# Load order, the queue of one load, and the source of the scaled identities at the start of a fused attention and feed-forward kernel

## Chip, cores, metric

One core of one Trainium2 chip. The metric is the device time of one execution in microseconds (us), as the median of several executions; lower is better. All executions told here count as fast in the record: none is over 1.5% above the fastest of its kernel.

## The reference, cut

```python
# q, k, v: (4, 8, 768, 64) fp32;  w_in: (512, 2048);  w_out: (2048, 512)
scores = scale * q @ k.T + (-slopes[h] * dist)     # ALiBi; window of 96 keys back, plus the 8 first keys
a = softmax(where(keep, scores, -1e9))
x = (a @ v).transpose(0, 2, 1, 3).reshape(3072, 512)
h = x @ w_in
out = (relu(h) ** 2) @ w_out                       # (3072, 512) fp32
```

## The kernel before

The sequence is cut into 24 tiles of 128 rows (T0 to T23), the feed-forward part into 12 blocks of two tiles with 8 steps each. A planner in the kernel's Python code decides at build time in which order each engine gets its operations, from estimated landing times. GpSimd issues nearly all loads, and they convert fp32 to bf16 on the way; SyncE loads the q and k of tile 0 in plain fp32. The weights come in 8 pieces each: i0 to i7 (w_in, named `win`) and o0 to o7 (w_out, named `wout`), 256 KB apiece in bf16.

```python
    issue = [1.0, 5.0]                     # the planner's estimate of issue and landing of the loads
    ...
    for j in range(NPLAIN):                # tile 0 only
        for n, src in ((0, q), (1, k)):
            t_ = const([P, d_model], FP32, f"plain_{n}{j}")
            nc.sync.dma_start(...)         # plain q, then plain k
            land["qk"[n], j] = 4.15 + 1.1 * n
    ...
    nc.gpsimd.iota(pbi, pattern=[[-P, 2], [-1, P]], base=0, channel_multiplier=1)
    load_part(0, 1)                        # q of tile 1, by GpSimd
    load_part(1, 1)                        # k of tile 1
    load_v(0)
    load_v(1)
    nc.scalar.activation(junk, zero[:, :1], Act.Exp)      # first exponential, result unused
    ...
    nc.vector.tensor_scalar(ident, pbi[:, 0, :], 0.0, None, op0=Alu.is_equal)   # bf16 identity
    ...
    for h in range(H):                     # 8 heads: identity times slope, the ALiBi term for TensorE
        nc.vector.tensor_scalar_mul(sid[h], ident, float(slopes[h] / scale))
    ...
    for w in "i0 T2 i1 T3 i2 o0 i3 o1 i4 o2 T4 i5 o3 i6 o4 T5 i7 o5 o6 o7".split():
        kind, n = w[0], int(w[1:])
        {"T": load_tile, "i": load_w_in, "o": load_w_out}[kind](n)     # T: q, k and v of a tile
    ...
    # last block: ScalarE copies each finished output part from PSUM, SyncE stores it
    nc.scalar.copy(o_sb[:, cols], acc);  nc.sync.dma_start(out=out[rows, cols], in_=o_sb[:, cols])
```

(The last line is condensed.)

The softmax here doesn't subtract the row's maximum and nothing guards it: scores larger than these inputs give would overflow.

Of the kernel before, what the change touches and what calls it, by code (L numbers as in the profile page):

```python
# [15 lines left out]
Alu = mybir.AluOpType  # L16
# [83 lines left out]
def kernel(  # L100
# [11 lines left out]
    nc = tc.nc  # L112
# [14 lines left out]
    scale = 1.0 / math.sqrt(D)  # L127
    slopes = [2.0 ** (-8.0 * (h + 1) / H) for h in range(H)]
# [20 lines left out]
    def const(shape, dt, name):  # L149
        return consts.tile(shape, dt, name=name, tag=name)  # L150
# [7 lines left out]
    ident = const([P, P], BF16, "ident")  # L158
# [3 lines left out]
    pbi = const([P, 2, P], I32, "pbi")  # L162
    pb = const([P, 2, P], BF16, "pb")
    pb0 = const([P, P], BF16, "pb0")
    sid = [const([P, P], BF16, f"sid_{h}") for h in range(H)]
# [10 lines left out]


    land = {}
    issue = [1.0, 5.0]

    def landed(name, at):
        land[name] = plan.op(("land",) + name, {"DMA": 0.0}, None, ready=at)
# [1 line left out]
    def slot(j):  # L184

        return j if j < NFIRST + 2 else NFIRST + 2 + j % NQ

    def src_rows(x, j):
        b, t = divmod(j, TPB)
        return x[b, :, t * P : (t + 1) * P, :]  # L190

    def swdge(name, dst, src, t):
        nc.gpsimd.dma_start(out=dst, in_=src)  # L193
        issue[1] = max(issue[1], issue[0] + 3.3) + t
        issue[0] += 0.75 if name[0][0] == "w" else 0.88

        land[name] = issue[1] + 0.3 + min(max(0.1 * (issue[1] - 8), 0.0), 1.6)

    plain = {}
    for j in range(NPLAIN):  # L200
        for n, src in ((0, q), (1, k)):
            t_ = const([P, d_model], FP32, f"plain_{n}{j}")
            nc.sync.dma_start(
                out=t_.rearrange("p (h d) -> p h d", h=H),
                in_=src_rows(src, j).rearrange("h p d -> p h d"),
            )
            plain[n, j] = t_
            land["qk"[n], j] = 4.15 + 1.1 * n


    def load_v(j):
        swdge(("v", j), v_sb[j][:, :, :D], src_rows(v, j).rearrange("h p d -> p h d"), 0.97)

    def load_part(n, j):
        swdge(
            ("qk"[n], j), qk_ring[slot(j)][:, n, :].rearrange("p (h d) -> p h d", h=H),
            src_rows((q, k)[n], j).rearrange("h p d -> p h d"), 0.85,
        )
# [6 lines left out]
    def load_w_in(s):  # L225
        f = slice(s * 2 * P, (s + 1) * 2 * P)
        swdge(
            ("win", s), w_in_sb[s],
            moe_w_in[:, f].rearrange("(km p) f -> p km f", p=P), 1.3,
        )  # L230
# [10 lines left out]
    def emit_ones(e, js):  # L241
        for j in js:
            nc.vector.memset(v_sb[j][:, :, D : D + 1], 1.0)

    emit_ones(None, range(NFIRST + 2))
    nc.gpsimd.iota(pbi, pattern=[[-P, 2], [-1, P]], base=0, channel_multiplier=1)  # L246
    load_part(0, 1)
    load_part(1, 1)
    load_v(0)
    load_v(1)  # L250

    nc.scalar.activation(junk, zero[:, :1], Act.Exp)

# [16 lines left out]
    nc.vector.memset(pb[:n_global, 1, :], float(-n_local))  # L270
    nc.vector.tensor_scalar_max(pb0[:n_global, :], pb0[:n_global, :], float(-n_local))
    for h in range(H):
        nc.vector.tensor_scalar_mul(sid[h], ident, float(slopes[h] / scale))
    for g in range(2):
        for odd in range(2):
            for i in range(2):
# [5 lines left out]
    for g in range(NFIRST + 2, NT, 6):  # L282
        js = range(g, min(g + 6, NT))
        o = plan.op(
            ("ones", g), {"DVE": 0.2}, lambda e, js=js: emit_ones(e, js),
            key=-1.0, ready=15.0,
        )
        ones.update({j: o for j in js})

    for w in "i0 T2 i1 T3 i2 o0 i3 o1 i4 o2 T4 i5 o3 i6 o4 T5 i7 o5 o6 o7".split():  # L290
        kind, n = w[0], int(w[1:])
        {"T": load_tile, "i": load_w_in, "o": load_w_out}[kind](n)
    for name, at in list(land.items()):
        landed(name, at)

# [36 lines left out]
    for j in range(NT):  # L332
# [61 lines left out]
        if j >= JQK:  # L394
            def emit_dT(e, j=j, T_=T_):
# [5 lines left out]
            T = plan.op(  # L401
                ("T", j), {"SP": 1.3}, emit_dT,
                deps=[land["q", j], land["k", j], xT_op[j - 3]] + ku, key=base - 6,
            )
            T = plan.op(("moved", j), {"DMAQ": 1.2}, None, deps=[T])
# [56 lines left out]
        for gs in [(0,), (1,)] if j < NSPLIT and not first else [tuple(range(groups))]:  # L462
            n = 8 * len(gs)
# [3 lines left out]
            if j < NBIAS:  # L467
# [6 lines left out]
            o = plan.op(  # L474
                ("sc", j, gs[0]), {"PE": 0.2 + 0.029 * n},
                lambda e, gs=gs, f=emit_sc: f(e, gs), deps=[*deps, bias],
                key=base + 1 + 2 * gs[0], takes=takes,
            )
# [237 lines left out]
    for o in plan.ops:  # L716
        if o["name"][0] == "sc":
            j = o["name"][1]
            n = 4 * j - LEAD
# [3 lines left out]
    for blk in range(NBLK):  # L723
# [9 lines left out]
        for s, sub, half in order2:  # L733
            users = acc_users.setdefault((sub, half), [])
            w = d_model if half is None else d_model // 2
# [3 lines left out]
            def emit_s2(e, blk=blk, s=s, sub=sub, half=half, w=w, cols=cols, own=own):  # L739
# [15 lines left out]
            o = plan.op(  # L755
                ("s2", blk, s, sub), {"PE": 0.43 * w / d_model}, emit_s2,
                deps=[d, land["wout", s]] + users[-1:],
                key=8 * blk + s + 2.0 + (0 if not last else 8 * sub + 8 * (half or 0)),
                takes=((*G, [users]) if own else ("acc", NACC, [users])) if s == 0 else None,
            )  # L760
# [71 lines left out]
```

## Time and profile before

| | before |
|---|---|
| time, median of 6 executions beside the changed kernel | 215.16 us (214.77 to 215.30) |
| span of the profiled execution | 213.1 us |
| TensorE busy | 205.5 us (96%) |
| last weight piece, o7, has landed | 41.97 us |
| last matmul ends | 209.96 us |
| from there to the end of the span | 3.1 us |

Times within a trace start at the span's start. A load's landing is when the last of its 16 DMA engines has finished. First the timeline of GpSimd in the kernel before (start, length, engine, line, operation, tiles): the jobs in which GpSimd writes the descriptors (the transfer orders for the DMA engines) for the v of tiles 0 and 1, joined into one row.

```profile
3.22 2.37 POOL L193 DMA_DIRECT2D v<-in_v_dram  x2
```

One by one in the trace, the first of the two took 1.50 us and the second 0.88. Then, in the DMA view, the 2.8 us that begin 0.34 us after the last matmul of before (210.3 to 213.1 us, the end of the span): the last store, 128 KB, by queue (packets, MB, share of the 16 engines), and its time from issue to landing.

```profile
q1 hardware_dynamic: 144, 0.13, 14.0%
...
out_dram<-o SPq DMA_DIRECT2D x1, 128.0 KB, 1.7
```

Nothing else uses the DMA engines there, and the store lands after 1.7 us.

### The profile page before, as it was taken

What the parts mean: (1) busy time and instruction counts of PE and PEld (TensorE: products, weight loads), DVE (VectorE), ACT (ScalarE), POOL (GpSimd) and SP (SyncE); (2) the same over time, 40 slices, a digit from 0 to 9 for tenths busy, and PEclk for the clock granted to TensorE, in tenths of its full rate; (3) what the DMA queues carried; (4) which work ended last, traced back from release to release, by engine and by line L of the source; (5) the groups of instructions that cost most, each with busy time, mean ns of one, the idle gap of its engine ahead of it and who ended that gap; (6) DMA issues with size and microseconds to landing.
All of it is one profiled execution on the core that took longest, in us unless ns stands there. A gap on an engine that the chain in (4) does not pass through costs nothing.

```text
span 213.1 us, 5046 instructions
## 1 busy us (share of the span) xinstructions
PE 205.5 (96%) x1992; PEld 141.2 (66%) x1992; DVE 142.4 (67%) x383; ACT 117.5 (55%) x217; POOL 74.4 (35%) x91
## 2 busy tenths in 40 slices
PE   7968999999999999999999999999999999999994
PEld 3656677655676767666767667666767667676773
DVE  7756668752886768755867957855857857844640
ACT  6848476633763645753654754753754754733541
POOL 8986677531044134314314422422422400000000
PEclk9999999999999999999999999999999999999999
DMA  9999999999899999999999899799999992310202
GB/s 127 140 165 197 182 196 182 178 123 210 185 95 87 218 100 93 189 129 84 203 141 81 180 103 119 154 128 119 192 130 78 152 131 39 123 28 0 98 0 98
DMA packets 113702, 27.58 MB, mean 129 GB/s; under 512 B 104336, under 2 KB 110736, under 8 KB 113680
## 3 DMA queue, kind: packets, MB, share of 16 engines
q0 software_dynamic: 79200, 13.37, 81.4%
q1 hardware_dynamic: 34480, 13.90, 32.7%
q8 instruction: 15, 0.25, 0.5%
q14 instruction: 7, 0.06, 0.1%
HBM read 27.26 MB, written 6.29 MB: 157 GB/s over the span
## 4 chain that ended last, share of the span: by engine, by line
PE 87%; DMA 7%; POOL 4%; issue 0%; ACT 0%; POOLq 0%
PE hT L675 39%; PE acc L745 38%; DMA win<-in_moe_w_in_dram 7%; PE sc L449 5%; PE po L562 4%; POOL qk L193 2%; POOL v L193 1%; PE tr L372 0%; POOL win L193 0%; PE trx L625 0%; ACT o L304 0%; POOL pbi L246 0%; POOLq L246 0%; POOLq L813 0%
## 5 line engine op out<-in xcount | busy, mean ns | idle before, releaser
L675 PE MATMUL hT<-xT,win 128*128 128x256 bf16 x768 | 98.7, 273 | 0.4 <-DMA win<-in_moe_w_in_dram 0.2
L745 PE MATMUL acc<-wout,hs 128*128 128x512 bf16 (+1 forms) x400 | 98.1, 371 | 0.2 <-DMA wout<-in_moe_w_out_dram 0.2
L696 ACT ACTIVATE hr<-hT 128x512 f32<-128x512 f32 x96 | 57.4, 599 | 68.1 <-PE hT L675 67.0
L675 PEld LDWEIGHTS <-win 128*128 128x128 bf16 x768 | 72.8, 98 | 23.9 <-DMA win<-in_moe_w_in_dram 1.6
L708 DVE TENSOR_TENSOR hs<-hr 128x512 bf16<-128x512 f32 x96 | 65.9, 687 | 23.0 <-ACT hr L696 21.7
L745 PEld LDWEIGHTS <-hs 128*128 128x128 bf16 x400 | 36.5, 98 | 24.4 <-issue 0.4
L193 POOL DMA_DIRECT2D qk<-in_q_dram x23 | 20.6, 894 | 87.0 <-DVE qk L346 75.0
L495 ACT ACTIVATE esc<-sc 128x512 bf16<-128x512 f32 x78 | 42.1, 601 | 10.3 <-PE sc L449 10.3
L520 DVE TENSOR_TENSOR at<-esc,E 128x512 bf16<-128x512 bf16 x78 | 32.0, 422 | 8.0 <-ACT esc L495 6.9
L193 POOL DMA_DIRECT2D v<-in_v_dram x24 | 22.2, 924 | 2.4 <-DVE at L520 1.2
L590 DVE TENSOR_TENSOR x<-po,rs 128x256 bf16<-128x256 f32 x48 | 20.4, 425 | 1.7
L193 POOL DMA_DIRECT2D qk<-in_k_dram x23 | 20.5, 892 | 0.3 <-issue 0.2
L562 PEld LDWEIGHTS <-at 128*128 128x128 bf16 x352 | 16.8, 97 | 4.5 <-ACT at L495 0.6
L562 PE MATMUL po<-v,at 128*128 128x65 bf16 x352 | 18.6, 193 | 0.3 <-ACT at L495 0.3
L589 DVE RECIPROCAL rs<-po 128x4 f32<-128x4 f32 x48 | 8.7, 181 | 13.2 <-PE po L562 13.0
L449 PEld LDWEIGHTS <-qkT 64*128 64x128 bf16 x352 | 9.9, 94 | 8.4 <-issue 6.6
L306 DVE COPY o<-acc 128x512 f32<-128x512 f32 x11 | 7.6, 692 | 10.6 <-PE acc L745 10.6
L449 PE MATMUL sc<-qkT 64*128 64x128 bf16 x192 | 13.1, 219 | 0.4 <-DVE qkT L306 0.3
L304 ACT COPY o<-acc 128x512 f32<-128x512 f32 (+1 forms) x14 | 7.8, 555 | 6.7 <-PE acc L745 6.7
L449 PE MATMUL sc<-qkT,qkT 64*128 64x128 bf16 x160 | 11.3, 216 | 0.0
L193 POOL DMA_DIRECT2D win<-in_moe_w_in_dram x8 | 6.4, 794 | 1.7 <-DMA win<-in_moe_w_in_dram 1.1
L495 ACT ACTIVATE at<-sc 128x512 bf16<-128x512 f32 x10 | 5.3, 598 | 2.5 <-PE sc L449 2.5
(41 smaller groups left out, 58.2 us busy)
## 6 DMA issues: line engine op xcount, KB each, us to landing
out_dram<-o SPq DMA_DIRECT2D x23, 256.0 KB, 3.1
v<-in_v_dram POOLq DMA_DIRECT2D x24, 128.0 KB, 5.6
qk<-in_q_dram POOLq DMA_DIRECT2D x23, 128.0 KB, 4.7
qk<-in_k_dram POOLq DMA_DIRECT2D x23, 128.0 KB, 5.4
win<-in_moe_w_in_dram POOLq DMA_DIRECT2D x8, 256.0 KB, 8.6
wout<-in_moe_w_out_dram POOLq DMA_DIRECT2D x8, 256.0 KB, 8.8
qkT<-qk SPq DMA_TRANSPOSE x18, 3.5
xT<-x SPq DMA_TRANSPOSE x18, 3.8
```

The source lines that it names most:

```text
L193: nc.gpsimd.dma_start(out=dst, in_=src)
L304: nc.scalar.copy(dst, src)
L449: nc.tensor.matmul(out=tiles["sc", j, odd, g][:, at, :], lhsT=qkT[(j - kt) % NKT][half, 1, pair, :], rhs=qkT[j % NKT][half, 0, pair, :], s ...
L495: nc.scalar.activation(out=esc, in_=tiles.pop(("sc", j, odd, g)).rearrange("p a c -> p (a c)"), func=Act.Exp, scale=scale,)
L520: nc.vector.tensor_mul(at, tiles.pop(("esc", j, odd, g)), bias)
L562: nc.tensor.matmul(out=po[:, hi, :], lhsT=tiles["at", j, odd, g][:, at * P : (at + 1) * P], rhs=v_sb[kj][:, h, :], start=(i == 0), stop=(i ...
L589: nc.vector.reciprocal(rs, po[:, :, D : D + 1])
L590: nc.vector.tensor_tensor(out=x[:, 4 * hf : 4 * hf + 4, :], in0=po[:, :, :D], in1=rs.to_broadcast([P, 4, D]), op=Alu.mult,)
L675: nc.tensor.matmul(out=hT[:, c, :], lhsT=w_in_sb[s][:, kt, c * P : (c + 1) * P], rhs=tiles["xT", blk][:, kt, :], start=(kt == 0), stop=(kt ...
L696: nc.scalar.activation(hr, tiles.pop(("hT", blk, s)), Act.Relu)
L708: nc.vector.tensor_mul(hs, hr, hr)
L745: nc.tensor.matmul(out=tiles["acc", blk, sub, half], lhsT=hs[:, c, sub * P : (sub + 1) * P], rhs=w_out_sb[s][:, c, cols], start=(s == 0 an ...
```

## The change

Its intent: to have the first four tiles on the chip before all weights but one, so that TensorE has attention work early; to get the k of tile 0 a little sooner by issuing it from a second queue; and to make the scaled identities straight from the int32 distances. The diff without its comments and blank lines:

```diff
-    issue = [1.0, 5.0]
+    issue = [1.35, 4.6]
-        land[name] = issue[1] + 0.3 + min(max(0.1 * (issue[1] - 8), 0.0), 1.6)
+        land[name] = issue[1] + (0.5 if issue[1] < 8 else 0.8 if issue[1] < 13.6 else 1.7)
-        for n, src in ((0, q), (1, k)):
+        for n, src, eng in ((0, q, nc.sync), (1, k, nc.scalar)):
-            nc.sync.dma_start(
+            eng.dma_start(
-            land["qk"[n], j] = 4.15 + 1.1 * n
+            land["qk"[n], j] = 4.15 + 0.6 * n
-    load_part(0, 1)
-    load_part(1, 1)
-    load_v(0)
-    load_v(1)
-        nc.vector.tensor_scalar_mul(sid[h], ident, float(slopes[h] / scale))
+        nc.vector.tensor_scalar(
+            sid[h], pbi[:, 0, :], 0.0, float(slopes[h] / scale), op0=Alu.is_equal, op1=Alu.mult
+        )
-    for w in "i0 T2 i1 T3 i2 o0 i3 o1 i4 o2 T4 i5 o3 i6 o4 T5 i7 o5 o6 o7".split():
-        kind, n = w[0], int(w[1:])
-        {"T": load_tile, "i": load_w_in, "o": load_w_out}[kind](n)
+    pieces = {
+        "T": load_tile, "i": load_w_in, "o": load_w_out, "v": load_v,
+        "q": lambda j: load_part(0, j), "k": lambda j: load_part(1, j),
+    }
+    for w in "q1 k1 v0 v1 q2 k2 v2 q3 k3 i0 v3 i1 i2 o0 i3 i4 T4 i5 o1 i6 o2 i7 o3 T5 o4 o5 o6 o7".split():
+        pieces[w[0]](int(w[1:]))
```

The first four loads are the same in both; `issue` and `land` are estimates by which the planner orders the work. "The new order" below always means the new order of loads together with the new estimates for GpSimd's loads.

## The prediction

> **What bounds the kernel now.** I read the page from the top: busy shares, slices, chain; then the chain in order of time, the waits and single issues of the first 45 us.
>
> ```profile
> span 213.1 us, 5046 instructions
> PE 205.5 (96%) x1992; PEld 141.2 (66%) x1992; DVE 142.4 (67%) x383; ACT 117.5 (55%) x217; POOL 74.4 (35%) x91
> ...
> PE   7968999999999999999999999999999999999994
> ...
> DMA  9999999999899999999999899799999992310202
> ...
> PE 87%; DMA 7%; POOL 4%; issue 0%; ACT 0%; POOLq 0%
> ```
>
> PE is busy for 205.5 of 213.1 us. The missing 7.6 us lie at the start (second digit row: slices 1 to 4, some 21 us) and in the last 3 us, when the last output is stored. The chain of waits, in order of time, says what the start waits for:
>
> ```profile
> 1.35 1.90 POOL qk L193 x2
> 3.25 2.34 POOL v L193 x2
> 5.59 0.76 POOL win L193
> 6.34 1.76 POOL qk L193 x2
> 8.10 0.82 POOL v L193
> 8.92 7.17 DMA win<-in_moe_w_in_dram
> 16.37 8.80 DMA win<-in_moe_w_in_dram
> 25.22 1.92 PE hT L675 x16
> ```
>
> Columns are start, length, what. Up to 25.22 us the chain is loads; from there it is matmuls to the end. So the time is "25.2 us, plus the PE work still to do then". The busy time by stretch (PE first after the length) shows where PE is short of work:
>
> ```profile
> 9.00:11.00 2.00, 1.63 (x29) 1.03 (x28) 1.47 (x7) 1.92 (x4) 2.00 (x3) 1.00 1.94 167
> 11.00:14.00 3.00, 1.52 (x24) 1.35 (x25) 1.19 (x5) 0.59 (x1) 3.00 (x5) 1.00 2.01 175
> 14.00:17.00 3.00, 2.79 (x39) 2.15 (x37) 1.83 (x22) 2.25 (x5) 1.90 (x3) 1.00 2.17 163
> 17.00:19.00 2.00, 1.55 (x34) 1.20 (x32) 1.31 (x5) 1.29 (x3) 1.75 (x3) 1.00 1.38 202
> 19.00:25.20 6.20, 5.74 (x62) 3.48 (x56) 5.48 (x16) 3.67 (x8) 3.97 (x5) 1.00 1.51 195
> 25.20:42.50 17.30, 17.28 (x185) 13.23 (x186) 12.60 (x29) 11.89 (x22) 11.49 (x14) 1.00 1.74 183
> ```
>
> Idle: 0.37 + 1.48 + 0.21 + 0.45 + 0.46 = 2.97 us between 9 and 25.2, then 0.02. The largest hole, in the timeline of PE, is tile 2, whose q and k stand behind a weight:
>
> ```profile
> 11.99 0.40 PE L372 MATMUL tr<-ident,qk 128*128 128x128 bf16 x4 [1.08 <-DMA qk<-in_q_dram]
> 12.87 0.40 PE L372 MATMUL tr<-ident,qk 128*128 128x128 bf16 x4 [0.48 <-DMA qk<-in_k_dram]
> ```
>
> Busy PE hides more, because a lone group shows its pipeline latency (four transposes 0.40 us, but 0.22 us apart when back to back). Counting the work from 4.15 to 25.2 us at the pace of back-to-back groups gives 14.2 us in 21, so about 7 us of PE is unused there. That is all a better start could ever win (3%).
>
> The DMA queue is the second bound. Landing times (issue plus time to landing, one issue at a time): q1 6.1, k1 6.8, v1 about 9.0; i0 11.1, q2 11.9, k2 12.8, v2 13.8; i1 16.1, q3 17.0, k3 17.7, v3 18.8; i2 20.0, o0 21.2, i3 22.6, o1 23.9, i4 25.2, o2 26.5; T4 27.4 to 29.2; i5 30.4, o3 31.6, i6 32.9, o4 34.3; T5 35.2 to 37.0; i7 38.2, o5 39.5, o6 40.7, o7 42.0 (i and o are the 256 KB pieces of the two weights, T a tile's q, k and v). Steady pace: 0.9 us for a q, k or v, 1.3 for a weight piece. It never pauses up to 42 us, and PE consumes o5 at 39.48 and o6 at 40.73 us, within 0.1 us of their landing. So even the smooth stretch after 25 us runs at the heels of the loads. Reordering can shift PE work in front of a late piece; it cannot make the last piece come much earlier.
>
> **What the Trainium skill says.** "DMA: Bandwidth & Descriptors", section "Issuing engines are not separate DMA queues": DMAs started from different engines run on the same 16 engines and interleave, so a second issuer only saves issue time. The trace agrees as far as it goes: tile 0's plain q and k are issued 0.52 us apart and land at 3.9 and 5.2 us, 1.3 us apart, so transfer and not issue separates them. "SBUF — State Buffer", section "Who interferes with whom": a VectorE tensor_scalar in a two-port mode locks GpSimd out, which then cannot write descriptors, and whoever starts first blocks the other. The trace has a case that fits: the first of the eight identity scalings took 585 ns and the median is 176, beside a running descriptor job. "VectorE: DVE Perf Modes", section "The perf-mode tier table": tensor_scalar runs at 4x from bf16 and 2x from fp32, so the int32 input of the new form should not be faster; at 128 columns that is a small part of 176 ns.
>
> **The change part by part.**
>
> *k of tile 0 on ScalarE's queue.* It is issued 0.52 us sooner, but both transfers share the engines. Their 2048 packets start at 2.9 us and moved at about 1,075 per us in the trace, so both should land near 2.9 + 1.9 = 4.8 us: k 0.4 earlier, q 0.9 later. The first transposes move from 4.15 to about 4.85 us, the second from 5.16 to 5.35. ScalarE's issue (about 0.5 us) is hidden, since its exponentials wait for the mask until 3.3 us anyway. Worth -0.2 us locally; tile 1's loads (6.1 and 6.8 us) are behind it and absorb that. Zero at the end.
>
> *Scaled identities from the distances.* Same eight instructions, 8 x 176 ns plus one stall = 1.3 us, ending near 4.7 us in both; first needed at 5.5 us. Zero.
>
> *Order of loads.* It removes i0 from ahead of T2 and i1 from ahead of T3; i1 to i4 follow v3, T4 comes two pieces earlier, and o1, o2, o3 later. Two gains. First, tile 2's and 3's q and k are no longer behind weights. A part lands 4.6 us after its issue where GpSimd is the limit, and issues are 0.88 us apart from 5.57 us: q2 10.2, k2 11.1, v2 12.0, q3 12.9, k3 13.8 instead of 11.9, 12.8, 13.8, 17.0, 17.7. Second, the queue runs with fewer holes: i0 + T2 took 4.8 us (9.0 to 13.8) and i1 + T3 took 5.0, where the steady pace gives 1.3 + 2.7 = 4.0. Of the excess 1.8 us, one 16 KB instruction fetch that held one DMA engine for 945 ns at 14.7 us explains about 1, and it will come again; a hole of about 0.5 us before i0's first packets will not. I credit 0.5 us. So i0 lands near 16.0 (after: 5 us later than before), i1 18.2, i2 19.5, o0 20.8, i3 22.1, i4 23.4, q4 24.3, i5 27.4, o1 28.7, i6 30.0, o2 31.3, i7 32.6, o3 33.9, k5 35.6, o4 37.7, o5 39.0, o6 40.2, o7 41.5.
>
> Now PE's new order (the order of the instructions is decided when the kernel is built, and can be read) against these, with 0.87 us a step of the first product (s1), 0.86 a step of the second (s2), 0.22 a transpose group, 0.24 a pv group, 0.55 a score group. All of tile 2's and 3's scores are done by about 16.3 us, then s1 0 with i0 at 16.0 to 16.3, s1 1 at 18.3 (i1), s1 2 at 19.6 (i2), s2 0 at 20.9 (o0), s1 3 at 22.2 (i3), s1 of block 1, s1 4 at 23.9. In the old order s1 4 starts at 25.22, with the same total in front of it (one s1 more, one s2 less). Ahead by 1.3 us there. Then the loads catch up: s2 1 waits for o1, 28.8; s1 6 for i6, 30.1; s2 2 for o2, 31.4; s2 6 for o6, 40.3; s2 7 about 41.7 to 41.9. In the old trace s2 7 starts at 42.46 with 0.24 us less work ahead of it, so it corresponds to 42.70: ahead by 0.8 to 1.0 us. The old stretch from 25.2 to 42.5 contained 0.4 us of small bubbles that my walk leaves out, so I take 0.4 to 1.0, centre 0.7. After 42 us nothing is changed but a few neighbours' places. 215.3 - 0.7 = 214.6 us.
>
> **Rivals.** (1) *The last weights bound everything:* o6 and o7 land as before (40.7, 42.0), the start's idle time only moves, and the gain is 42.70 - 42.1 = 0.6 at most, likelier 0.2: 215.1. For it: PE takes o5 and o6 at their landing. (2) *The loads recover both excesses*, i1 to o7 land 1.1 us earlier, and PE follows: 213.8. For it: no weight among parts, no hole; against it: the instruction fetch. (3) *First product late:* i0 lands 5 us later and four s1 steps bunch behind 16 us; with too little attention work to fill, PE idles from 16.5 to 22 and the new order starts behind: 215.6. For it: s1 1, s1 2, s2 0 and s1 3 each wait for a landing in my walk. (4) *Attention at once fills the gap*, all 3 us of idle time gone: 212.5; against it the landings from 18 us on.
>
> **Range and chances.** The rivals span 213.8 to 215.6, centre 214.6; 8 in 10 for 213.9 to 215.3. Two per cent would be 4.3 us, more than all visible idle time before 25 us; nor does anything here cost that.
>
> **What would show it.** Right: waits for q2 and q3 shrink from 1.08 us to a few tenths; PE waits for win and wout between 16 and 32 us instead; i4 near 23.4; o7 near 41.5; the chain still loads first, then matmuls from some point between 20 and 42 us. Wrong: o7 a whole us earlier or later than 41.5, plain q still landing at 3.9, sid instructions longer than 0.3 us each, or a PE wait on ACT or VectorE that replaces the loads before 25 us.

## The result

The changed kernel took 215.56 us (215.49 to 216.72, 6 executions), the kernel before 215.16. The ratio is 1.0035, with a 95% interval of 1.0013 to 1.0056: not faster, but about 0.35% (0.75 us) slower. The predicted 214.6 and its range up to 215.3 miss it. (Ratios here are the mean time of one kernel's fast runs over that of the other's of the same rounds, so not quite the ratio of the medians quoted.) The profiled execution happened to be the slowest of the six, 216.72 us. A second run of the same kernel (e1_again) gave a profile at 215.28, which is typical.

The page of the changed kernel, top lines and chain:

```profile
span 214.9 us, 5049 instructions
PE 206.4 (96%) x1992; PEld 142.0 (66%) x1992; DVE 142.6 (66%) x384; ACT 117.3 (55%) x216; POOL 74.8 (35%) x91
...
PE   7988999899999999999999999999999999999992
...
DMA  8999999999796999997999999899999990310202
...
PE 82%; DMA 9%; POOL 6%; DVE 0%; issue 0%; ACT 0%; POOLq 0%
```

The first slices of PE are fuller (7988 for 7968), but PE's total share has not moved, and DMA's part of the chain has grown from 7% to 9%. The chain of waits of the changed kernel, in order of time:

```profile
1.35 1.89 POOL qk L193 x2
3.24 2.68 POOL v L193 x2
5.92 1.75 POOL qk L193 x2
...
14.14 8.99 DMA win<-in_moe_w_in_dram
23.18 2.79 PE hT L676 x24
...
29.86 9.88 DMA wout<-in_moe_w_out_dram
39.79 1.02 PE acc L746 x4
```

Compare the second line with the chain of before: the jobs for v take 2.68 us in place of 2.34. And in this execution a weight piece of the second product still ends a wait at 39.79 us, where the chain of before had left its last load at 25.22. The timeline of PE in the changed kernel, waits only:

```profile
14.38 0.40 PE L373 MATMUL tr<-ident,qk 128*128 128x128 bf16 x4 [0.46 <-DMA qk<-in_k_dram]
...
16.26 1.05 PE L676 MATMUL hT<-xT,win 128*128 128x256 bf16 x8 [0.28 <-DMA win<-in_moe_w_in_dram]
19.17 1.05 PE L676 MATMUL hT<-xT,win 128*128 128x256 bf16 x8 [0.51 <-DMA win<-in_moe_w_in_dram]
20.51 1.05 PE L676 MATMUL hT<-xT,win 128*128 128x256 bf16 x8 [0.29 <-DMA win<-in_moe_w_in_dram]
39.79 1.02 PE L746 MATMUL acc<-wout,hs 128*128 128x512 bf16 x4 [0.89 <-DMA wout<-in_moe_w_out_dram]
```

The waits for q and k of tile 2 (1.08 and 0.48 us) are gone, as intended. Waits for weights at 16 to 21 us stand in their place, as the prediction's walk had them; e1_again shows none over 0.15 us there, but a wait of 0.19 us for the k of tile 2 and a long one for the k of tile 3, shown under its heading. The wait of 0.89 us at 39.79 us belongs to this slow execution; e1_again has none there. The busy time by stretch of e1_again (columns as in the prediction):

```profile
11.00:14.00 3.00, 2.60 (x52) 2.22 (x52) 2.10 (x9) 2.12 (x5) 3.00 (x5) 1.00 1.93 154
14.00:17.00 3.00, 1.78 (x33) 1.45 (x34) 1.66 (x18) 1.40 (x3) 2.80 (x5) 1.00 1.63 167
```

From 11 to 14 us PE does 1.08 us more than before, from 14 to 17 us 1.01 us less. Most of the idle time has moved; over the whole of 9 to 25.2 us it is 2.28 us in this view, where it was 2.97 before.

Now the two views from above. GpSimd's timeline in the changed kernel, the jobs for v:

```profile
3.22 2.69 POOL L193 DMA_DIRECT2D v<-in_v_dram  x2
```

The first job is 1.82 us long in place of 1.50, and the next load is issued 0.33 us later than in before. The same 2.8 us after the last matmul of the changed kernel (211.3 to 214.1 us) in the DMA view:

```profile
q1 hardware_dynamic: 144, 0.13, 14.0%
q14 instruction: 1, 0.01, 1.6%
...
out_dram<-o SPq DMA_DIRECT2D x1, 128.0 KB, 2.5
```

An instruction fetch of 8 KB has come into the last store, and the store takes 2.5 us in place of 1.7. The three parts of the time:

| | before | changed | changed, e1_again |
|---|---|---|---|
| o7 landed, us | 41.97 | 43.58 | 42.00 |
| from there to the last matmul's end | 168.0 | 167.4 | 167.5 |
| last matmul's end | 209.96 | 210.96 | 209.52 |
| tail to the end of the span | 3.1 | 3.9 | 3.7 |

So the new order does leave about 0.5 us less to do after o7, but o7 has not come sooner and the tail is 0.6 to 0.8 us longer. That o7 comes no sooner was the prediction's rival 1; the longer tail is nowhere in it.

### The profile page after: what moved, and what is told of

Same layout as the page of the kernel before. It is cut to its first block, busy times and chain, and to the rows that moved or that the text cites. A ratio compares the mean times of both kernels' runs of the same rounds, so it can differ in the third digit from the quotient of the medians.

```text
span 214.9 us, 5049 instructions
## 1 busy us (share of the span) xinstructions
PE 206.4 (96%) x1992; PEld 142.0 (66%) x1992; DVE 142.6 (66%) x384; ACT 117.3 (55%) x216; POOL 74.8 (35%) x91
## 3 DMA queue, kind: packets, MB, share of 16 engines
q1 hardware_dynamic: 33440, 13.64, 31.6%
## 4 chain that ended last, share of the span: by engine, by line
PE 82%; DMA 9%; POOL 6%; DVE 0%; issue 0%; ACT 0%; POOLq 0%
PE acc L746 37%; PE hT L676 35%; PE sc L450 5%; DMA wout<-in_moe_w_out_dram 5%; DMA win<-in_moe_w_in_dram 4%; PE po L563 4%; POOL qk L193 3%; POOL v L193 2%; POOL win L193 1%; POOL wout L193 0%; PE tr L373 0%; DVE hs L709 0%; ACT o L305 0%; POOL pbi L246 0%; PE trx L626 0%
## 5 line engine op out<-in xcount | busy, mean ns | idle before, releaser
L676 PE MATMUL hT<-xT,win 128*128 128x256 bf16 x768 | 97.7, 273 | 1.2 <-DMA win<-in_moe_w_in_dram 1.1
L496 ACT ACTIVATE esc<-sc 128x512 bf16<-128x512 f32 x78 | 41.5, 605 | 6.9 <-PE sc L450 6.7
L521 DVE TENSOR_TENSOR at<-esc,E 128x512 bf16<-128x512 bf16 x78 | 32.1, 422 | 10.2 <-ACT esc L496 8.6
L305 ACT COPY o<-acc 128x512 f32<-128x512 f32 (+1 forms) x15 | 8.3, 560 | 8.1 <-PE acc L746 8.1
L307 DVE COPY o<-acc 128x512 f32<-128x512 f32 x10 | 6.9, 692 | 7.6 <-PE acc L746 7.6
L193 POOL DMA_DIRECT2D wout<-in_moe_w_out_dram x8 | 5.7, 707 | 3.0 <-DMA win<-in_moe_w_in_dram 2.2
```

The lines of the kernel that those rows point to most:

```text
L193: nc.gpsimd.dma_start(out=dst, in_=src)
L305: nc.scalar.copy(dst, src)
L496: nc.scalar.activation(out=esc, in_=tiles.pop(("sc", j, odd, g)).rearrange("p a c -> p (a c)"), func=Act.Exp, scale=scale,)
L521: nc.vector.tensor_mul(at, tiles.pop(("esc", j, odd, g)), bias)
L676: nc.tensor.matmul(out=hT[:, c, :], lhsT=w_in_sb[s][:, kt, c * P : (c + 1) * P], rhs=tiles["xT", blk][:, kt, :], start=(kt == 0), stop=(kt ...
```

## The experiments

Theory at the start: the order of loads gains some tenths; the int32 identities lose some by keeping GpSimd from writing descriptors; k on ScalarE's queue loses or does nothing. Rival: the order itself gains nothing, because the last pieces land when they land. Each part was then undone or done alone. What was found on the way (the fetch in the last store) made a second theory, tested by the last four runs.

All runs in one table. All outputs are right. "Fetch" says whether an 8 KB instruction fetch fell into the last store's packets; "v job" is GpSimd's first v job; o7 and tail are of the one profiled execution; the ratio is to the kernel before on the same chip.

| run | order | identities | k on | median us | ratio [95%] | v job | o7 | tail | fetch |
|---|---|---|---|---|---|---|---|---|---|
| e1_again | new | int32 | ScalarE | 215.48 | 1.0042 [1.0018, 1.0066] | 1.83 | 42.00 | 3.7 | yes |
| e2_order_only | new | bf16 | SyncE | 214.14 | 0.9976 [0.9951, 1.0002] | 1.50 | 41.07 | 3.2 | no |
| e3_no_sid | new | bf16 | ScalarE | 214.67 | 1.0005 [0.9983, 1.0027] | 1.50 | 41.86 | 4.0 | yes |
| e4_no_k | new | int32 | SyncE | 214.81 | 1.0014 [0.9990, 1.0038] | 1.83 | 41.79 | 3.2 | no |
| e5_sid_only | old | int32 | SyncE | 215.16 | 1.0015 [0.9990, 1.0040] | 1.83 | 41.95 | 3.1 | no |
| e6_k_only | old | bf16 | ScalarE | 214.71 | 0.9992 [0.9970, 1.0014] | 1.49 | 41.30 | 3.1 | no |
| e7_order_stt | new | two bf16 | SyncE | 213.63 | 0.9946 [0.9922, 0.9969] | 0.90 | 40.61 | 3.2 | no |
| e8_order_again | new | bf16 | SyncE | 214.59 | 0.9987 [0.9962, 1.0012] | 1.50 | 41.81 | 3.2 | no |
| e9_order_k_stt | new | two bf16 | ScalarE | 214.22 | 0.9968 [0.9943, 0.9993] | 0.90 | 40.76 | 3.8 | yes |
| e10_order_stt_again | new | two bf16 | SyncE | 213.36 | 0.9923 [0.9901, 0.9946] | 0.90 | 40.64 | 3.2 | no |
| e11_before_stt | old | two bf16 | SyncE | 213.89 | 0.9958 [0.9926, 0.9991] | 0.90 | 40.88 | 3.1 | no |
| e12_order_k_again | new | bf16 | ScalarE | 215.39 | 1.0021 [0.9994, 1.0049] | 1.50 | 42.31 | 3.7 | yes |
| e13_order_stt_plus1 | new | two bf16 | SyncE, one more exp | 214.10 | 0.9959 [0.9937, 0.9981] | 0.90 | 40.41 | 4.1 | yes |
| e14_order_k_stt_minus1 | new | two bf16 | ScalarE, one exp less | 213.55 | 0.9933 [0.9914, 0.9953] | 0.90 | 40.72 | 3.2 | no |
| e15_after_minus1 | new | int32 | ScalarE, one exp less | 214.85 | 0.9993 [0.9968, 1.0017] | 1.83 | 42.02 | 3.2 | no |
| e16_order_stt_third | new | two bf16 | SyncE | 213.62 | 0.9930 [0.9909, 0.9951] | 0.90 | 41.14 | 3.2 | no |

### e1_again

Edit: none, the changed kernel as it is.

> The changed kernel unaltered, for a second profile. In the first one a q, k or v load (v of tile 5) took 2.4 us instead of 1.0 on one lagging DMA engine, and PE then waited 0.95 us for weight piece o4; that execution was also the slowest of six (216.72 us against a median of 215.56). Theory S (supply: the end moves with the landing of weight pieces, which the new order does not make earlier): without that second lag the wait for o4 is below 0.4 us, i1 lands near 19 us, i3 near 23 us, span 213.4 to 213.9, time 215.4 to 215.7. Rival C (cold start: tile 0's transposes ran at half the TensorE pace up to 6.2 us because q came 0.6 us later): this is a matter of phase and some executions will be without it, with times up to 0.8 us lower.

Measured: 1.0042, the loss again. It is real, and the slow profile of the first run is not its cause: here no weight is waited for at 39 us. But k of tile 3 is, 1.58 us:

```profile
15.18 0.40 PE L373 MATMUL tr<-ident,qk 128*128 128x128 bf16 x4 [1.58 <-DMA qk<-in_k_dram]
```

(PE's timeline of e1_again.) A 16 KB instruction fetch of 1,194 ns started at 11.86 us, in the middle of that load, and the last of the load's 16 DMA engines then came 0.82 us behind the fifteenth. Rival C does not hold: tile 0's transposes start 0.21 us apart in the first profile and 0.11 us apart in e1_again, where the clock record at full speed begins at 4.5 us and not at 6.4, and still that execution took 215.28 us. The slow pace comes with k on SyncE too (e4, e10), and e10 has the lowest median of all runs.

### e2_order_only and e8_order_again

Edit, against the changed kernel:

```diff
-        for n, src, eng in ((0, q, nc.sync), (1, k, nc.scalar)):
+        for n, src, eng in ((0, q, nc.sync), (1, k, nc.sync)):
-            land["qk"[n], j] = 4.15 + 0.6 * n
+            land["qk"[n], j] = 4.15 + 1.1 * n
-        nc.vector.tensor_scalar(
-            sid[h], pbi[:, 0, :], 0.0, float(slopes[h] / scale), op0=Alu.is_equal, op1=Alu.mult
-        )
+        nc.vector.tensor_scalar_mul(sid[h], ident, float(slopes[h] / scale))
```

> The new order of loads and the planner's new estimates alone; k of tile 0 back on SyncE's queue, identities scaled from the bf16 identity again. Theory S: the order itself gives nothing, 215.1 to 215.4, ratio 0.999 to 1.002; GpSimd's first v job 1.5 us long again instead of 1.8. Rival C: the order is worth 0.5 us or more and the other two parts spoil it, 214.3 to 214.8, ratio 0.995 to 0.998.

> The new order alone once more, beside the others on this chip and for a second profile: ratio to the kernel before 0.996 to 0.999 if its gain is real. If the profiled execution has one DMA engine lagging by 1.5 us or more from 13 us on, it is 0.6 to 0.9 us slower than one without, within the same kernel.

Measured: 0.9976 and 0.9987, each alone not clear of 1. Together about 0.2% less, some 0.4 us. The rival, that the new order gains nothing, is not excluded by these two; e7, e10 and e16 against e11 point the same way. How much of this gain is left when the clock is looked at is told under the grid.

### e3_no_sid and e12_order_k_again

Edit: the changed kernel with the identities made as before.

```diff
-        nc.vector.tensor_scalar(
-            sid[h], pbi[:, 0, :], 0.0, float(slopes[h] / scale), op0=Alu.is_equal, op1=Alu.mult
-        )
+        nc.vector.tensor_scalar_mul(sid[h], ident, float(slopes[h] / scale))
```

> The changed kernel with the identities scaled from the bf16 identity as before. Theory S with a lock between VectorE and GpSimd: GpSimd's job for v of tile 0 goes from 1.82 back to 1.50 us, every later load is issued 0.3 us earlier, weight pieces land 0.3 us earlier, time 0.2 to 0.3 us below the changed kernel (215.2 to 215.4). Rival: the longer job was absorbed, no difference to the changed kernel within 0.1 us.

> New order and k of tile 0 on ScalarE, identities from the bf16 identity, again and on this chip: ratio 0.999 to 1.002 as in its first run; if k on ScalarE costs nothing, 0.997 to 0.999 as for the order alone.

Measured: 1.0005 and 1.0021, against 0.9976 and 0.9987 of the same order with k on SyncE. So k on ScalarE costs about 0.3%. The tail shows where: 4.0 and 3.7 us against 3.2. Against e1_again, which has int32 identities, e3 is 0.8 us faster, more than the 0.2 to 0.3 us expected.

### e4_no_k

Edit: the changed kernel with k back on SyncE.

```diff
-        for n, src, eng in ((0, q, nc.sync), (1, k, nc.scalar)):
+        for n, src, eng in ((0, q, nc.sync), (1, k, nc.sync)):
-            land["qk"[n], j] = 4.15 + 0.6 * n
+            land["qk"[n], j] = 4.15 + 1.1 * n
```

> The changed kernel with k of tile 0 back on SyncE's queue. Theory S: plain q lands at 3.96 instead of 4.59 us, the first transposes start at 4.4 and at the fast TensorE pace, but the queue of loads behind is the same: time within 0.1 us of the changed kernel. Rival C: 0.3 us or more faster than the changed kernel.

Measured: 1.0014, tail 3.2 us. Against the order alone the int32 identities cost, against the whole change k's removal gains: 0.67 us on the medians, where theory S had expected at most 0.1. Rival C named such a size, but its reason does not hold: tile 0's first transposes are at the slow pace here too (0.21 us apart).

### e5_sid_only and e6_k_only

Edits: the kernel before with one part of the diff alone.

```diff
 e5
-        nc.vector.tensor_scalar_mul(sid[h], ident, float(slopes[h] / scale))
+        nc.vector.tensor_scalar(
+            sid[h], pbi[:, 0, :], 0.0, float(slopes[h] / scale), op0=Alu.is_equal, op1=Alu.mult
+        )
 e6
-        for n, src in ((0, q), (1, k)):
+        for n, src, eng in ((0, q, nc.sync), (1, k, nc.scalar)):
-            nc.sync.dma_start(
+            eng.dma_start(
-            land["qk"[n], j] = 4.15 + 1.1 * n
+            land["qk"[n], j] = 4.15 + 0.6 * n
```

> The kernel before with nothing changed but the identities, now made from the int32 distances. Lock theory (eight two-port VectorE instructions in a row keep GpSimd from writing descriptors until the last is done): GpSimd's job for v of tile 0 takes 1.83 us instead of 1.50, later jobs are issued 0.33 us later, time +0.3 to +0.7 us against the kernel before (ratio 1.0015 to 1.0035). Rival (it only hurts together with the new order): ratio 0.999 to 1.001.

> The kernel before with nothing changed but k of tile 0 issued by ScalarE. If the cost of 0.5 to 0.7 us that it had beside the new order is its own (q of tile 0 lands 0.6 us later, k no earlier): ratio 1.002 to 1.003. If it needs the new order: ratio 0.999 to 1.001, since tile 2's loads (11.9 us) are behind it in the old order.

Measured: 1.0015 for the identities, with an interval that reaches below 1, and 0.9992 for k. The v job in e5 is 1.83 us, as in the changed kernel. That e6 costs nothing was the surprise: if the transfer from ScalarE's queue did harm by itself, it should do so here too. Its tail is 3.1 us.

### e7_order_stt, e10_order_stt_again, e11_before_stt

If the v job is long because VectorE's identities lock GpSimd out, then another way of making them should free it. "SBUF — State Buffer", section "Who interferes with whom", infers that an operation with two inputs from SBUF takes only the read interface of the shared pair and leaves the write interface, which descriptors need. So the identity was multiplied by the slope and by itself:

```diff
-        nc.vector.tensor_scalar_mul(sid[h], ident, float(slopes[h] / scale))
+        nc.vector.scalar_tensor_tensor(
+            out=sid[h], in0=ident, scalar=float(slopes[h] / scale), in1=ident,
+            op0=Alu.mult, op1=Alu.mult,
+        )
```

in the version of e2 (e7, e10) and in the kernel before (e11).

> The new order alone, and the identities made by a two-input VectorE instruction (scalar_tensor_tensor of the identity with itself), which should not take the port that GpSimd writes descriptors through, though each instruction is longer. Lock theory: v of tile 0's job falls from 1.50 to about 0.9 us, its successors are issued 0.5 us earlier, time 0.3 to 0.6 us below the order alone. Rival (GpSimd's job is long for a reason of its own): job stays at 1.5 us or more, no gain or a loss.

> New order and two-input identities again: ratio to the kernel before 0.993 to 0.997 if the gain of 0.5% is real; GpSimd's job for v of tile 0 0.9 us.

> The kernel before with two-input identities and nothing else. Lock theory: every load from v of tile 1 on is issued 0.5 to 0.6 us earlier; if the end moves with the landing of weight pieces it gains 0.4 to 0.6 us (ratio 0.997 to 0.998) and the new order adds 0.4 us to that. Rival: the lock hurts only where loads of q and k follow one another and GpSimd is the limit (new order), and here the gain is below 0.2 us.

Measured: 0.9946, 0.9923, and 0.9958 with the old order. The v job is as the lock theory had it; the gain is larger than it had it (about 1 us from e8 to e7 where 0.3 to 0.6 was expected, and 0.9958 where 0.997 to 0.998 was). The view of the instructions that touch `sid`, in before, in the changed kernel, and in the third run of this version, e16 (count, ns min/median/max, first and last start):

```profile
L273 DVE TENSOR_SCALAR sid<-ident x8: 175/176/585, 3.4 to 4.1; 128x128 bf16<-128x128 bf16 x8
```

```profile
L269 DVE TENSOR_SCALAR sid<-pbi x8: 206/206/208, 3.4 to 4.4; 128x128 bf16<-128x128 int32 x8
```

```profile
L269 DVE SCALAR_TENSOR_TENSOR sid<-ident x8: 271/272/273, 3.4 to 4.8; 128x128 bf16<-128x128 bf16 x8
```

and GpSimd's timeline of e16 beside them:

```profile
3.21 1.78 POOL L193 DMA_DIRECT2D v<-in_v_dram  x2
4.94 0.92 POOL L193 DMA_DIRECT2D qk<-in_q_dram  x1
```

The slowest instruction is the best neighbour. With 176 ns operations GpSimd got in before the eighth, which then took 585 ns, and its first v job was 1.50 us long. With 206 ns operations none of the eight was held up, all ran back to back to 4.56 us, and GpSimd waited until then: 1.82 us. With the two-input form no job waits for another: 0.90 us for the first v job, and q2 (the first new-order load behind v) is issued at 4.94 us in place of 5.90 in the changed kernel.

### e9_order_k_stt

Edit: e7's version with k on ScalarE.

> New order, two-input identities, and k of tile 0 on ScalarE's queue. If k on ScalarE costs 0.6 us of its own beside the new order (as the first two pairs of runs suggest): 0.4 to 0.8 us slower than the same kernel with k on SyncE. If those pairs were scatter of the lagging DMA engine: within 0.2 us of it.

Measured: 0.9968, tail 3.8 us; e10 on the same chip had 0.9923 and 3.2. The cost of k stands beside this form of the identities too, and it lies in the tail.

### e13 to e16: what in k's move costs at the end

In every version with a long tail the last store was one DMA engine short. Fifteen of the 16 engines were done 2.1 us after the last matmul in all kernels; in the long ones the sixteenth came at 2.7 to 3.2 us, and an 8 KB fetch of instructions on queue 14 started among the store's packets, 1.5 to 2.0 us after the last matmul. In the others the same fetch came 3.5 us or later after the last matmul, behind the store. What the versions with a long tail had in common was the length of ScalarE's program: 322 instructions of it in the traces of all of them, 321 for the new order with k on SyncE, 318 for k alone and 317 in the kernel before. (So four of the five more come with the new order.) A queue that fetches a block when the program reaches a certain place would make 322 the trouble, not k. Two theories: the count, or the transfer of k. e13 is e7's version (k on SyncE) with one more instruction; e14 and e15 keep k on ScalarE and drop one.

```diff
 e13, in e7's version
     nc.scalar.activation(junk, zero[:, :1], Act.Exp)
+    nc.scalar.activation(junk, zero[:, :1], Act.Exp)
 e14, in e9's version, and e15, in the changed kernel
-    nc.scalar.activation(junk, zero[:, :1], Act.Exp)
```

> New order, identities by scalar_tensor_tensor, k on SyncE, and one more tiny exponential on ScalarE at the start (its result is used by nothing). If the number of ScalarE's instructions decides where the fetch falls: the time from the last matmul to the end of the span goes from 3.2 to 3.7 to 4.0 us, an 8 KB fetch starts about 1.5 us after the last matmul, and the time is 0.4 to 0.7 us above e16 (ratio to before 0.995 to 0.998). If the k transfer itself is the cause: tail 3.2 us, same time as e16 within 0.3 us.

> The version of e9 (new order, k on ScalarE, scalar_tensor_tensor) without the small exponential at ScalarE's start. Instruction count: tail 3.2 us in place of 3.8, time as e16 within 0.3 us (ratio to before 0.992 to 0.995). The k transfer itself: tail stays 3.7 to 4.0 us, ratio 0.996 to 0.999.

> The changed kernel itself without the small exponential at ScalarE's start. Instruction count: tail 3.2 us in place of 3.7 to 3.9, time 214.8 to 215.0 (ratio to before 1.000 to 1.002). The k transfer itself: nothing changes, ratio 1.003 to 1.005, tail 3.7 to 3.9 us.

> Repeat of e7 and e10 (213.4 to 213.6 us, ratio to before 0.992 to 0.995), as the standard for the three others of this call. Both theories expect the same of it.

Measured: e13 0.9959 against 0.9930 of e16; e14 0.9933; e15 0.9993, against 1.0035 and 1.0042 of the changed kernel. The count decides, in both directions, and the transfer of k does nothing at the end. (That queue 14 serves ScalarE's program is concluded from this, no view says it.) e15 came out just under the 1.000 to 1.002 expected. The same 2.8 us after the last matmul in the DMA view of e13 (k on SyncE, one instruction more):

```profile
q14 instruction: 1, 0.01, 0.7%
...
out_dram<-o SPq DMA_DIRECT2D x1, 128.0 KB, 2.7
```

and of e15 (k on ScalarE, one instruction less than the changed kernel):

```profile
q1 hardware_dynamic: 144, 0.13, 14.1%
...
out_dram<-o SPq DMA_DIRECT2D x1, 128.0 KB, 1.7
```

e13's tail of 4.1 us was a little over the 3.7 to 4.0 expected, and its fetch came 2.0 us after the last matmul rather than 1.5. The page itself carries the mark: queue 14 has 8 packets in every version that pays and 7 in every other one, here the changed kernel and e15:

```profile
q14 instruction: 8, 0.07, 0.1%
```

```profile
q14 instruction: 7, 0.06, 0.1%
```

### The runs as a grid

The versions with the new order, as mean ratios of the rows of the table (the changed kernel's first run, 1.0035, included):

| identities | fetch behind the store | fetch in the store | cost of the fetch |
|---|---|---|---|
| bf16 (e2, e8; e3, e12) | 0.9982 | 1.0013 | 0.31% |
| int32 (e4, e15; first run, e1) | 1.0004 | 1.0039 | 0.35% |
| two bf16 (e7, e10, e14, e16; e9, e13) | 0.9933 | 0.9964 | 0.31% |

The two effects add up cleanly. Of 215 us, the fetch costs 0.66 to 0.75 us, and int32 against bf16 identities 0.22 to 0.26%, some 0.5 us. The two-input form gains 0.49%, 1.05 us, over the bf16 form. The old order has 1 (before), 1.0015 (e5) and 0.9958 (e11) where the new one has 0.9982, 1.0004 and 0.9933: the new order gains 0.18%, 0.11% and 0.25%, a mean of 0.39 us. The three parts of the change make -0.4 + 0.5 + 0.7 = +0.8 us; measured were 0.75 (ratio 1.0035) and 0.9 (1.0042). The runs of the whole change are themselves in the grid; without them, from the bf16 row for order and fetch and from e4 and e15 for the identities, the sum is -0.40 + 0.47 + 0.67 = +0.74 us.

One difference between executions was not part of any theory, and it bears on the smallest of the three numbers. Beside the runs e1 to e16, 17 of 44 executions of the kernel before have a mean granted clock of 0.992, and so have 2 of the 18 of e5, e6 and e11; of the 78 with the new order, 4 have. A mean of 0.992 is what one stretch of 3.41 us at half clock makes in 213 us, and the three profiles with such a mean (e5, e8, e12) have that stretch between 14.3 and 20.1 us. Here it is in e8, in the view by stretch (the third figure from the end is the granted clock):

```profile
16.40:19.70 3.30, 3.30 (x32) 2.13 (x29) 2.26 (x24) 2.14 (x5) 2.45 (x4) 0.50 1.38 199
```

The executions of before with such a mean were 0.5 to 0.8 us longer than its others. If all executions with it are left out, the new order gains 0.08%, 0.07% and 0.07% in the three rows, some 0.15 us, while the fetch (0.27 to 0.39%), int32 against bf16 (0.2 to 0.3%) and the two-input form (0.5%) stay about what they were. So more than half of the 0.39 us comes from how often the stretch fell into the executions compared. Whether its fuller start prevents the stretch was not tested, and neither figure is clear of noise in a single run.

The version of e7, e10 and e16 (new order, k on SyncE, two-input identities) beats both kernels: 213.4 to 213.6 us, 0.5 to 0.8% under the kernel before by its three ratios, and e14 shows that k may as well be issued by ScalarE if the instruction count stays below the bad one.

## Why the prediction was wrong, point by point

The prediction's sum was -0.7 for the order, 0 for the identities and 0 for k. The runs put -0.15 to -0.4, +0.5 and +0.7 in their places. The two zeros are what turned a gain into a loss.

**The order of loads: direction right, its size too large.** Ahead in order was right: the work left after o7 went from 168.0 to 167.5 us, 0.5 us (0.6 in the first profile). The credited 0.5 us of earlier landings was not there: o7 was predicted at 41.5 us and landed at 42.00 in e1_again. The queue should have been issuing q2 at 5.57 us; it did at 5.90. In the two profiles of the changed kernel q2 landed at 10.07 and 10.39 us and k2 at 10.92 and 11.23, close to the 10.2 and 11.1 of the prediction, but i1 at 18.63 and i4 at 23.93 were 0.4 to 0.5 us late in e1_again (i1 0.9 and i4 1.0 in the first profile). The order by itself came out nearest to the prediction's rival 1, "likelier 0.2".

**The scaled identities: wrong.** "Eight instructions, ending near 4.7 us in both, zero." The end was about right (4.56 us in place of 4.70), and beside the point. The cost does not lie in when `sid` is ready but in what VectorE keeps GpSimd from doing: the v job is 0.33 us longer, and the whole supply moves. The prediction quoted the page on this lock and drew no conclusion for the new form. It also took the 585 ns for the first of the eight instructions; the trace has it at the eighth (4.12 to 4.70 us), which is the one that GpSimd got in front of. That the int32 form would be no faster was right: 206 ns against 176. e4, e15 and the first run against the bf16 versions give about 0.5 us. That this exceeds the 0.33 us of the job, and that the two-input form gains 1.05 us where the job is only 0.60 shorter, is not settled; the mean o7 moves by more than the job too (40.7 us over the seven two-input profiles, 41.7 over the six bf16 ones with before), and where the instruction fetches strike differs.

**k on ScalarE's queue: "zero at the end" was wrong, by a path that was not among the rivals.** It costs 0.7 us at the end of the kernel, and it is no property of the transfer: one instruction more in ScalarE's program moves an 8 KB instruction fetch into the last store. e13 makes the cost without k, e14 and e15 have k without the cost. At the start, "both near 4.8 us" was half right: plain q landed at 4.43 to 4.79 us over the versions with it, plain k at 5.01 to 5.37, where they had landed at 3.97 and 5.11 before (1.14 us apart, not the 1.3 of the prediction). The "0.2 us locally" was not seen either. The estimate counted the packets from 2.9 us; in the trace of before they start at 1.86 us on the clock of the views. That was an error of 1.04 us in reading, and the fetch that the prediction puts at 14.7 us started at 13.64.

**What bounds the kernel: right in the main.** The prediction put the time at 25.2 us plus PE's work, and the loads second; the runs turn this round. The time is the landing of the last weight piece plus a nearly fixed amount of work plus the tail. In all 14 profiles of the new order the last matmul ends 167.4 to 167.9 us after o7; with the old order it is 167.9 to 168.0 us, and 168.6 in e5, whose profile has the half-clock stretch. Rival 1, the last weights bound everything, was the best description of the supply. Rival 3 gave the right number, 215.6, by luck: PE does wait at 16 to 21 us, but that is not where the time is lost, since versions with the same order are faster.

**The profiled execution.** Its 43.58 us for o7 comes on top. One DMA engine lagged behind the other 15: the last piece of the load of v5 came at 39.05 us, on the second-last engine it had been there at 36.91, and a 16 KB fetch of 974 ns had started at 36.46 us (the trace does not say on which engine). This was one of the prediction's signs of being wrong, o7 a whole us off 41.5; e1_again does not show it. In e2 and e8, the same kernel, the lag of the last engine up to o7 is at most 0.5 and 1.5 us, o7 is at 41.07 and 41.81 and the times of the profiled executions are 213.69 and 214.88. This fits a lag that is carried along once a fetch has hit an engine that is already behind. But e8's profile also has the half-clock stretch, so the pair does not show which of the two makes the difference, or the spread of about 1 us between executions of one kernel. No experiment was made on it.

## What to carry to other kernels

Where GpSimd writes descriptors at the start, look at what VectorE does at the same time, and judge an operation by how long GpSimd's jobs become, not by its own duration: 272 ns operations beat 176 and 206 ns ones. Before crediting or blaming a change for some tenths of a per cent, split the time into supply, work and tail, compare the queues' packet counts and the executions' granted clocks: one instruction more or less can move an instruction fetch into the last store. When parts of a change are small, do each alone and together, and see whether they add up.

## What the Trainium skill lacked or had wrong

- "Runtime: NRT & Kernel Launch", section "Instruction fetch mechanics", calls the cost of crossing a block boundary "mostly hidden" and gives blocks of 16 KiB. Here the records show fetches of 16 KB on queue 8 and of 8 KB on queue 14. One of 8 KB in the last store made the store 2.2 to 2.7 us instead of 1.7 and the kernel 0.7 us slower; those of 16 KB took 0.9 to 1.7 us each while the loads up to o7 ran.
- The same section has the fetches come at block boundaries, counted in instructions (256 a block). What neither it nor another page that I found says is that one instruction more or less (322 or 321 on ScalarE) can so move a fetch into the last store and cost or save 0.3%.
- "SBUF — State Buffer", section "Who interferes with whom", marks as inferred that an operation with two SBUF inputs leaves GpSimd's descriptor writing alone. The runs bear it out: a descriptor job of 0.90 us beside eight scalar_tensor_tensor operations, 1.50 us beside tensor_scalar from bf16, 1.82 us beside tensor_scalar from int32. The same section says that whoever starts first blocks the other. It could add that the back-to-back run matters: of eight operations of 206 ns GpSimd got in between none, of eight of 176 ns before the eighth.
